# Block-sparse attention and feed-forward kernel: mask tiles built by two concurrent 64-row products, chunk 1 masked by multiplies instead of by TensorE

## The chip, the cores and the metric

The kernel runs on one core of one Trainium2 chip. The metric is the device time of one execution in microseconds, as the median of several executions. The kernel before was run beside every kernel on the same chip. A run over 1.5% above the fastest run of its own kernel is called slow, the others fast; a slow run is left out of the ratios, and no argument should rest on it alone. In the records the engines are called PE (TensorE), DVE (VectorE), ACT (ScalarE), POOL (GpSimd) and SP (SyncE). Run labels such as e1 name the experiments below; the numbers e4 and e5 were not run.

## The reference, cut to what matters

```python
# q, k, v: (4, 8, 768, 64) float32; sampled_blocks: (24, 3)
scores = scale * np.matmul(q, k.transpose(0, 1, 3, 2))
mask = near-diagonal, first and last rows and columns of 32-blocks, plus three sampled blocks a row
attn = softmax(np.where(mask, scores, -1e9))
x = heads_side_by_side(attn @ v)                 # 3072 tokens of 512
xn = x / sqrt(mean(x * x) + 1e-6) * rms_g
out = (silu(xn @ w_gate) * (xn @ w_val)) @ w_out # 512 -> 1536 -> 512
```

The kernel works in 12 chunks of 256 query rows, three for each of four batches. Each chunk has 12 score tiles, exponentials, a mask, the value products, a row normalisation (sum of squares, a reciprocal root, a scaling), transposes, and then the feed-forward products (192 a chunk, 2,304 in all).

## The kernel before: what the change and the argument touch

The mask is put on in one of two ways. For the first `PMASK` pairs of heads (`PEM` is true), TensorE adds a large negative number to the scores by a second product. For all others the exponentials are multiplied by a tile of zeros and ones, `Mk`, made on TensorE by `mask_tile` and copied out by `mask_copy`.

```python
PMASK = 8
def PEM(ch, pr):
    return ch * NP + pr < PMASK            # 8: chunks 0 and 1; 4: chunk 0

def scores(t):
    ...
    nc.tensor.matmul(out=s_, lhsT=x[rows, 1, ...], rhs=x[rows, 0, ...], start=True, stop=not PEM(ch, pr))
    if PEM(ch, pr):
        nc.tensor.matmul(out=s_, lhsT=KindG[rows, ...], rhs=NegQ[rows, ...], start=False, stop=True)

def mask_tile(ic, j2):
    mps[ic, j2] = mp = fbank()             # one PSUM bank
    for j in range(2):
        nc.tensor.matmul(out=mp[:, j * CQ:(j + 1) * CQ], lhsT=KindG[0:64, 2 * j2 + j, :],
                         rhs=NegQ[0:64, cols], start=True, stop=True)

def mask_(t, e):                           # the multiply, on VectorE or GpSimd
    (nc.gpsimd if e == "POOL" else nc.vector).tensor_tensor(
        out=pv, in0=pv, in1=m..., op=ALU.mult)

def rstd(ch):                              # reciprocal root of the row sums, on GpSimd
    nc.gpsimd.tensor_tensor(out=rs, in0=mss[ch], in1=nhalf, op=ALU.pow)

def scale_x(ch, qt):                       # row scaling, on VectorE, two instructions
    for lo, n in ((0, DM), (DM, D)):       # 512 columns and 64 columns
        nc.vector.scalar_tensor_tensor(
            out=x2[:, lo:lo + n], in0=x1s[ch][:, qt, 0:n], scalar=mss[ch][:, qt:qt + 1],
            in1=gB[:, 0:n], op0=ALU.mult, op1=ALU.mult)

def load_stage(b, i):                      # queries, keys, values of batch 1 and up: one buffer for all
    stages[b, i] = raw.tile([P, H, NC * D], FP32, name="stage", tag="stage", bufs=1)
```

Every engine works its instructions off in the order of one long list of words, `ORDER`. In it `m1_0_2*POOL` is a mask multiply of chunk 1 on GpSimd, `sc0_0` a row scaling of chunk 0, `rs0` its reciprocal root, `w5` a pair of idle matmuls, `l1_0_0` half the query load of batch 1, `c1_0_0` one of its casts out of the staging buffer, `va1_0` one of the casts of its values.

The softmax here doesn't subtract the row's maximum and nothing guards it: scores larger than these inputs give would overflow.

## Time and profile before

| | before |
|---|---|
| median of 4 executions beside the changed kernel | 293.5 us (292.52 to 294.8) |
| span of the profiled execution, mean granted clock | 292.3 us, 1.000 |
| first feed-forward product | 30.97 us |
| row scaling of chunk 0 on VectorE, start and length | 26.51 us, 1.81 us |
| query load of batch 1 issued by GpSimd | 42.54 us |

### The profile page before, as it was taken

The page shows a single profiled execution, that of the slowest core. Times are in us where ns is not written, and L with a number is a line of the kernel's source. Part 1 is how long each engine was busy: PE and PEld are TensorE (multiplying, and loading weights), DVE is VectorE, ACT ScalarE, POOL GpSimd, SP SyncE. Part 2 cuts the span into 40 slices and gives each one's busy share as a digit, 9 for nine tenths or more (in the row PEclk, how much of TensorE's full clock was granted, in tenths as well). Part 3 has the DMA queues.
Part 4 walks back from the last instruction along what each step waited for, and adds up shares of the span by engine and source line. Part 5 has one row for each costly group of instructions (what it writes and reads, how often), then busy time and mean ns, then how long its engine had stood idle before and what let it go on. Part 6 is the DMA issues. An engine that isn't in the chain of part 4 may idle for free.

```text
span 292.3 us, 10748 instructions
## 1 busy us (share of the span) xinstructions
PE 284.6 (97%) x4579; PEld 221.1 (76%) x4605; DVE 237.9 (81%) x486; ACT 227.6 (78%) x462; POOL 44.6 (15%) x66
## 2 busy tenths in 40 slices
PE   8999999999999999999999999999999999999995
PEld 4677889965489788686787687688686797776872
DVE  5448298999999999989999979998969788966370
ACT  6899958999999998788599599699399498543312
POOL 9530031726021230001020020000000000000000
PEclk9999999999999999999999999999999999999999
DMA  8999989995875799913679379142051032023203
GB/s 180 311 204 206 292 154 243 172 286 156 186 237 152 185 200 231 168 66 75 220 150 183 103 113 162 21 67 82 2 109 39 3 70 76 2 44 105 74 2 108
DMA packets 56692, 39.76 MB, mean 136 GB/s; under 512 B 42244, under 2 KB 50052, under 8 KB 56644
## 3 DMA queue, kind: packets, MB, share of 16 engines
q1 hardware_dynamic: 45268, 17.11, 33.1%
q0 software_dynamic: 10688, 21.50, 29.4%
q8 instruction: 36, 0.59, 0.9%
q10 hardware_dynamic: 688, 0.46, 0.5%
q14 instruction: 12, 0.10, 0.1%
HBM read 28.57 MB, written 6.29 MB: 119 GB/s over the span
## 4 chain that ended last, share of the span: by engine, by line
PE 83%; DVE 10%; ACT 3%; issue 3%; POOL 0%; POOLq 0%; ACTq 0%; DVEq 0%
PE f L836 37%; PE f L869 19%; PE f L649 10%; PE f L679 10%; DVE pt L669 4%; DVE uu L847 2%; PE f L654 2%; PE f L321 2%; ACT pt L662 2%; DVE hp L854 2%; PE f L484 1%; DVE X L693 1%; DVE x L718 1%; PE f L733 1%; ACT junk L704 0%
## 5 line engine op out<-in xcount | busy, mean ns | idle before, releaser
L662 ACT ACTIVATE pt<-f 128x512 bf16<-128x512 f32 x288 | 151.8, 636 | 8.6 <-PE f L649 7.1
L836 PE MATMUL f<-xn,wgv 64*128 64x256 bf16 x2304 | 139.2, 269 | 0.4 <-DVE uu L847 0.3
L836 PEld LDWEIGHTS <-wgv 64*128 64x128 bf16 x2304 | 117.0, 94 | 11.9 <-issue 2.6
L669 DVE TENSOR_TENSOR pt<-pt,Mk 128x1024 bf16<-128x1024 bf16 x120 | 77.8, 696 | 0.7 <-ACT pt L662 0.7
L869 PE MATMUL f<-wo,hp 128*128 128x512 bf16 (+1 forms) x274 | 65.7, 370 | 1.9 <-issue 0.8
L847 DVE SCALAR_TENSOR_TENSOR uu<-th,f 128x512 bf16<-128x512 bf16 x72 | 48.8, 682 | 12.9 <-ACT th L843 12.6
L843 ACT ACTIVATE th<-f 128x512 bf16<-128x512 f32 x72 | 44.1, 615 | 16.6 <-PE f L836 16.1
L649 PE MATMUL f<-qkT 64*128 64x256 bf16 x576 | 56.5, 273 | 0.5 <-ACT qkT L490 0.2
L854 DVE TENSOR_TENSOR hp<-uu,f 128x512 bf16<-128x512 bf16 x72 | 48.6, 684 | 4.2 <-PE f L836 0.5
L869 PEld LDWEIGHTS <-hp 128*128 128x128 bf16 x300 | 26.1, 98 | 28.2 <-issue 5.1
L679 PEld LDWEIGHTS <-pt 128*128 128x128 bf16 x1152 | 38.4, 97 | 6.8 <-issue 1.1
L679 PE MATMUL f<-va,pt 128*128 128x65 bf16 x1152 | 40.0, 193 | 0.1
L649 PEld LDWEIGHTS <-qkT 64*128 64x128 bf16 x576 | 29.8, 95 | 11.0 <-issue 7.8
L712 POOL TENSOR_TENSOR rs<-ms,nhalf 128x2 f32<-128x2 f32 x12 | 9.8, 816 | 160.9 <-ACT junk L704 127.3
L718 DVE SCALAR_TENSOR_TENSOR x<-X,rs,gB 128x512 bf16<-128x512 f32 (+1 forms) x48 | 22.0, 513 | 10.7 <-POOL rs L712 10.5
L704 ACT ACTIVATE junk<-X 128x513 bf16<-128x513 f32 x22 | 13.8, 636 | 21.6 <-DVE X L693 21.5
L891 ACT ACTIVATE yo<-f 128x512 f32<-128x512 f32 (+1 forms) x24 | 13.4, 607 | 10.8 <-PE f L869 10.8
L693 DVE TENSOR_TENSOR X<-f,rz 128x256 f32<-128x256 f32 x48 | 20.4, 425 | 1.7
L654 PE MATMUL f<-NegQ,KindG 64*128 64x256 bf16 x96 | 13.3, 287 | 0.0
L691 DVE RECIPROCAL rz<-f 128x4 f32<-128x4 f32 x48 | 8.4, 176 | 4.8 <-PE f L679 4.5
L275 POOL DMA_DIRECT2D stage<-in_v_dram x8 | 6.2, 776 | 11.1 <-ACT qb L269 8.5
L269 DVE CAST va<-stage 128x768 bf16<-128x768 f32 x11 | 5.7, 554 | 2.6 <-DMA stage<-in_v_dram 2.6
(82 smaller groups left out, 111.9 us busy)
## 6 DMA issues: line engine op xcount, KB each, us to landing
stage<-in_v_dram POOLq DMA_DIRECT2D x8, 768.0 KB, 7.5
out_dram<-yo SPq DMA_DIRECT2D x23, 256.0 KB, 2.3
stage<-in_k_dram POOLq DMA_DIRECT2D x6, 768.0 KB, 8.8
stage<-in_q_dram POOLq DMA_DIRECT2D x6, 768.0 KB, 6.1
wgv<-in_moe_w_gate_dram POOLq DMA_DIRECT2D x3, 512.0 KB, 17.4
wgv<-in_moe_w_val_dram POOLq DMA_DIRECT2D x3, 512.0 KB, 18.6
wo<-in_moe_w_out_dram POOLq DMA_DIRECT2D x2, 768.0 KB, 17.4
xn<-x SPq DMA_TRANSPOSE x40, 3.3
```

The source lines that it names most:

```text
L649: nc.tensor.matmul(out=s_, lhsT=x[rows, 1, 2 * j2 + jj, pr, :], rhs=x[rows, 0, 2 * ic:2 * ic + 2, pr, :], start=True, stop=not PEM(ch, pr))
L654: nc.tensor.matmul(out=s_, lhsT=KindG[rows, 2 * j2 + jj, :], rhs=NegQ[rows, ic * CQ:(ic + 1) * CQ], start=False, stop=True)
L662: nc.scalar.activation(out=pts[ch, pr][:, j2, e], in_=st[t][e], func=AF.Exp, scale=SCALE)
L669: (nc.gpsimd if e == "POOL" else nc.vector).tensor_tensor(out=pv, in0=pv, in1=m.unsqueeze(1).to_broadcast([P, 2, 2 * CQ]), op=ALU.mult)
L679: nc.tensor.matmul(out=o_[:, qt, e, 0:D + 1], lhsT=pt[:, jt // 2, e, jt % 2 * CQ + qt * P:jt % 2 * CQ + (qt + 1) * P], rhs=va[(ch // NIC) ...
L693: nc.vector.tensor_tensor(out=x1s[ch][:, :, 2 * pr * D:(2 * pr + 2) * D].rearrange("p t (h d) -> p t h d", h=2), in0=o4[:, :, :, 0:D], in1 ...
L718: nc.vector.scalar_tensor_tensor(out=x2[:, lo:lo + n], in0=x1s[ch][:, qt, 0:n], scalar=mss[ch][:, qt:qt + 1], in1=gB[:, 0:n], op0=ALU.mult ...
L836: nc.tensor.matmul(out=gst[u, fp, name][:, half * CQ:(half + 1) * CQ], lhsT=wgv[rows, dpart(i, c), f * P:(f + 1) * P], rhs=xns[u][rows, c, :],
L843: nc.scalar.activation(out=ths[u, fp], in_=gst[u, fp, "gp"], func=AF.Tanh, scale=0.5)
L847: nc.vector.scalar_tensor_tensor(out=uus[u, fp], in0=ths.pop((u, fp)), scalar=1.0, in1=gst.pop((u, fp, "gp")), op0=ALU.add, op1=ALU.mult)
L854: nc.vector.tensor_tensor(out=hps[u][:, 2 * fp:2 * fp + 2, :].rearrange("p f t -> p (f t)"), in0=uus.pop((u, fp)), in1=gst.pop((u, fp, "vp ...
L869: nc.tensor.matmul(out=yst[u, t, half][:, 0:n], lhsT=hps[u][:, f, t * P:(t + 1) * P], rhs=wo[:, f, cols], start=(f == 0), stop=(f == NF - 1))
```

## The change

The aim is to use both halves of the array for mask tiles (two products at a time, into two banks), to take chunk 1's mask products off TensorE (`PMASK` 8 to 4), and to put idle matmuls only where the opening leaves wide gaps. Three of the twelve new multiplies of chunk 1 go to GpSimd. The whole order was made anew. Cut to its core:

```diff
-    PMASK = 8
+    PMASK = 4
-    FILL = 6
+    FILL = 13
-    def mask_tile(ic, j2):
-        mps[ic, j2] = mp = fbank()
-        for j in range(2):
-            nc.tensor.matmul(out=mp[:, ...], lhsT=KindG[0:64, 2 * j2 + j, :], rhs=NegQ[0:64, cols], ...)
+    def mask_tiles(g):
+        for i in range(2):
+            mps[g, i] = fbank()
+        for n in range(4 * g, min(4 * g + 4, NM)):
+            i, (ic, c) = n % 2, divmod(n, NC)
+            rows = slice(64 * i, 64 * i + 64)
+            nc.tensor.matmul(out=mps[g, i][:, ...], lhsT=KindG[rows, c, :], rhs=NegQ[rows, ...], ...)
 ORDER (words of the new one; many left out)
+... rs0 one1 wv2_ ... m1_0_0*DVE m1_0_1*DVE sc0_0:0 sc0_1:1 ... xt0_0:60 w7:5 xt0_1:5 ... sta1_1 ...
+l1_1_0 l1_1_4 m1_0_2*POOL h0_0:0 m1_1_1*POOL wo0_ ... m1_3_1*POOL ...
+sq1_0*ACT sq1_1*ACT c1_1_0*DVE ... sta1_0 dt1_1_0 rs1 l1_0_0 l1_0_4 wo1_ c1_0_0*POOL ...
+... sta1_2 l1_2_0 l1_2_4 va1_0*POOL va1_1*POOL va1_2*POOL va1_3*POOL ... l2_1_0 rs2 l2_1_4 ...
```

## The prediction

> **What bounds the kernel now.** I read the page's busy shares first, then stretches of the span, then the chain and the timeline of the opening.
>
> ```profile
> PE 284.6 (97%) x4579; PEld 221.1 (76%) x4605; DVE 237.9 (81%) x486; ACT 227.6 (78%) x462; POOL 44.6 (15%) x66
> ```
>
> A busy TensorE (PE) is not a TensorE at its peak, so the 97% has to be read by stage. The stretches (start:end, length, then busy us and instruction count of each engine):
>
> ```profile
> 8.00:17.00 9.00, 8.80 (x123) 5.48 (x121) 3.79 (x9) 8.29 (x17) 3.72 (x6) 1.00 1.18 290
> 17.00:31.00 14.00, 13.92 (x284) 11.35 (x283) 8.69 (x24) 13.82 (x29) 2.82 (x4) 1.00 1.24 207
> 31.00:40.00 9.00, 8.87 (x192) 8.11 (x188) 4.17 (x11) 6.34 (x14) 0.00 (x0) 1.00 1.13 276
> 40.00:55.00 15.00, 15.00 (x273) 14.13 (x269) 13.73 (x26) 12.79 (x25) 6.03 (x9) 1.00 0.95 194
> 55.00:85.00 30.00, 29.09 (x418) 19.14 (x418) 29.50 (x60) 29.78 (x63) 11.31 (x14) 1.00 0.85 193
> 110.00:200.00 90.00, 89.26 (x1492) 70.30 (x1498) 83.43 (x164) 74.89 (x153) 6.02 (x8) 1.00 0.72 132
> ```
>
> The order of the columns is PE, weight loads, VectorE (DVE), ScalarE (ACT), GpSimd (POOL). Until 31 us ScalarE is full (13.82 of 14.00) with the exponentials of chunks 0 and 1, and VectorE has 5 us free; from 31 to 40 VectorE has another 5 us free. From 55 to 85 VectorE and ScalarE are both full and TensorE waits a little; after 110 TensorE leads. The first feed-forward product stands at 30.97 us. From there TensorE always has some product in reserve, so the time is roughly that start, plus all TensorE work left then, plus gaps. How that start comes about (the chain, start, length, what):
>
> ```profile
> 27.55 0.55 PE f L733 x8
> 28.11 0.73 PE f L679 x24
> 28.84 0.45 PE f L733 x8
> ...
> 30.73 0.59 ACT pt L662
> 31.33 0.04 issue
> 31.37 2.78 PE f L836 x47
> ```
>
> Between the two batches of transposes (L733) of chunk 0's normalised rows lies one attention-value product of chunk 1 (0.73 us); four score tiles with their mask products fill 29.28 to 30.73 before the first product.
>
> The groups that the change touches (busy us, mean ns):
>
> ```profile
> L654 PE MATMUL f<-NegQ,KindG 64*128 64x256 bf16 x96 | 13.3, 287 | 0.0
> L321 PE MATMUL f<-idle 128*128 128x256 bf16 x26 | 5.8, 373 | 1.1 <-DVE idle L296 1.1
> L559 PE MATMUL f<-NegQ,KindG 64*128 64x256 bf16 x18 | 3.4, 269 | 0.0
> ```
>
> Means are latencies, not costs. Costs come from the chain: "0.11 PE f L654 x2" is 54.5 ns for one mask product when two of different row halves run together, "0.87 PE f L836 x16" gives the same, and 24 value products take 0.73 us. The mask-tile products (L559) use rows 0 to 63 only, and the second starts 0.11 us after the first, so each costs 109 ns.
>
> **What the Trainium skill says.** "TensorEngine Tiling (Array Packing)", Gotcha 1 (PSUM Pressure): different row tiles write different PSUM banks and can't use one bank at the same time. So pairing needs the two banks that the change takes. The trace agrees as far as it goes: the score and mask pairs of two row halves go to two banks and cost 54.5 ns each.
> "TensorE: Matmul & The Clock Gate", Part 1: the array runs at half rate until a window of about 3.4 us has been busy. The trace agrees: the 14 first idle matmuls take 3.17 us, 226 ns each; a pair of score products starts every 0.21 us until 10.1 us and every 0.11 us from 11.9 us.
> "VectorE: DVE Perf Modes", the perf-mode tier table: a bf16 two-tensor product runs two elements a cycle from SBUF, anything fp32 from PSUM one. The trace has 682 ns for the 1024-wide mask multiply and 682 ns for the 512-wide mask copy, issued about 0.61 us apart.
> "GPSIMD Engine Reference", section 3.1 (Elementwise), puts GpSimd about two times slower than VectorE for two-input work. No instruction of this trace shows a wide two-input product there.
>
> **The change, part by part.**
> *Mask products of chunk 1.* 48 of the 96 leave TensorE: 48 x 54.5 ns = 2.6 us. Nearly all lie before 31 us (only the last tile's four follow the first product: 4 x 54.5 = 0.22 us). There ScalarE sets the pace: a tile needs 2 x 0.506 = 1.01 us of exponentials (13 took 6.58 us), against 0.44 us of TensorE with the mask. So the 2.6 us are worth little by themselves; they turn into gaps, which is why the new order has idle matmuls there.
> *Mask tiles.* Before, 18 x 109 ns = 1.96 us, all between 46 and 83 us, where TensorE counts. After, 9 pairs, 0.98 us; by the new order four pairs move before the first product, and five remain, 0.55 us. On the path: -1.41 us.
> *Mask copies.* Before six on VectorE and three on ScalarE, all after 46 us. After, four of 512 columns go into the opening, and the late ones are three of 512 and one of 256 on VectorE, one of each on ScalarE. VectorE's late stretch loses (6 - 3.5) x 0.61 = 1.5 us, ScalarE's (3 - 1.5) x 0.57 = 0.85 us.
> *Mask multiplies of chunk 1.* Twelve more: nine on VectorE, 9 x 0.61 = 5.5 us, three on GpSimd, for which I assume about 2 us each (an estimate from twice the time on VectorE, with issue). Two stand in the wait for the reciprocal root (0.72 us on GpSimd), the other seven, 4.3 us, fall where VectorE was 4.8 us free (31 to 40 us). They should not push the full stretch after 40.
> *Idle matmuls.* 14 more, each about 0.11 us, 1.5 us if none fell into a gap. By the order, nine pairs precede the first product and four follow; those four cost 4 x 0.22 = 0.88 us at worst and nothing at best. None now stands in the first 12 us, where two pairs of the old ones were.
> *Order.* The whole order is new. Chunk 0's exponentials had 1.75 us of evacuations between them on ScalarE (gaps at 11.33, 14.59 and 15.88 us); now one small evacuation and one mask copy, about 0.95 us: -0.8, and about -0.1 for two copies taken off ScalarE ahead of the first exponential. Later, the value product between the two transposes is gone: -0.75. The two multiplies in the root's wait cost about +0.4 (1.2 us against 0.8). Sum -1.25: first product at about 29.7 us. But two score tiles (0.44), that value product (0.73) and one small mask product (0.11) now come after it.
>
> TensorE's work after the first product: 0.44 + 0.73 + 0.11 + 0.55 - 0.22 - 1.96 = -0.35 us, if the late idle matmuls fall in gaps.
> Gaps: in 55 to 85 us TensorE's records are 68 products (3.7), 46 output products of about 0.229 (10.5), 104 scores (5.7), 205 value products of 0.0305 (6.3) and 14 mask-tile products (1.5), 27.7 us of 30, so 2.3 us are gaps. With 1.5 us of VectorE and 0.85 of ScalarE gone, I give back 1.0.
> Sum: -1.25 - 0.35 - 1.0 = -2.6, and 293.4 - 2.6 = 290.8 us.
>
> **Rivals.**
> 1. *The array stays cold longer.* Without idle matmuls early, the window that now turns the clock at about 10.2 us may miss, and the next is 3.4 us later. Four score tiles would cost 0.87 us instead of 0.44, transposes half as much again; ScalarE would idle about 1.5 us. For it: the clock turned only after an unbroken run of scores and idle matmuls. Against: three score tiles still run back to back, and ScalarE has slack against TensorE once started. Result about 292.5.
> 2. *VectorE becomes the bound earlier.* Chunk 1's values now wait for multiplies on VectorE and the slow GpSimd ones, and TensorE takes them in order. If these run late or slow each other, work spills into the stretch after 40 us. For it: VectorE is 92% full from 40 us on. Against: 10 us are free before. Result 293 to 295.
> 3. *Everything removed is hidden anyway*, as the 2.6 us are: then only the 1.4 us of mask tiles count, less idle matmuls: 292.5.
> 4. *The new order packs better everywhere.* TensorE's gaps outside the stretches named come to some 6 us (from 31 to 289 us: 2304 products at 54.6 ns, 125.8; 276 output products at 216 ns and 24 half ones, 62.2; 121 score tiles at 0.218, 26.4; 43 value products at 0.727, 31.3; the rest 3.5; so 249 of 258, 9 us of gaps, less the 2.3). An order that closes half of them gives 288. Nothing in the diff speaks for that in particular.
>
> **Range and chances.** The central sum is small and its largest terms (start of the first product, gaps) come from the order, not from the removed work. Each is uncertain by about 1 us; rivals 1 and 3 lie above, rival 4 below. I take 288.3 to 293.3. Faster by over 2% means under 287.5, which needs rival 4 on top of the sum: 0.10. Slower by over 2% means over 299.2: 0.01. Within 2%: 0.89.
>
> **What would show it.** Right: the first product near 29.7 us; L559's pairs starting together; late mask copies down to six; VectorE fuller in 17 to 40 us and not over 98% after; the last chunk-0 exponential by about 21.9 us. Wrong: scores 0.21 us apart after 11 us (rival 1); TensorE waiting for the mask multiply before chunk 1's values (rival 2); a first product no earlier and the same gaps in 55 to 85 us (rival 3); a gain that lies after 110 us (rival 4).

## More of the kernel before

The lines of the profile stand in the prediction. One that it does not show is the row scaling, from VectorE's timeline:

```profile
26.51 1.81 DVE L718 SCALAR_TENSOR_TENSOR x<-X,rs,gB 128x512 bf16<-128x512 f32 x4 [0.18 <-POOL rs L712]
```

Another line, which the prediction did not use, already held a warning. It is the row of the mask multiplies of the kernel before between 45 and 110 us, with the durations as least, median and greatest, in ns:

```profile
L669 DVE TENSOR_TENSOR pt<-pt,Mk x37: 679/682/1305, 52.3 to 104.3; 128x1024 bf16<-128x1024 bf16 x37
```

Nearly all take 682 ns; the greatest takes 1,305. Only four take over 720 ns, and all four start while GpSimd casts: two, 1,000 and 1,050 ns, beside the query casts of batch 1 (52 to 57 us), and two, 870 and 1,305 ns, beside its value casts (63 to 69 us).

## The result, and the profile after

| | before | after |
|---|---|---|
| median | 293.5 us (292.52 to 294.8), 4 runs | 301.04 us (300.22 to 301.95), 4 runs |
| profiled span, mean granted clock | 292.3 us, 1.000 | 300.2 us, 0.988 |
| first feed-forward product | 30.97 us | 34.96 us |

All runs of both are fast. The ratio is 1.0255 with a 95% interval of 1.0205 to 1.0305: the changed kernel is slower. Ratios in this document are the mean time of one kernel's fast runs over that of the other's of the same rounds, so they are not quite the ratio of the medians quoted.

From the page of the changed kernel, the busy shares and the granted clock by slices of 7.5 us:

```profile
PE 287.6 (96%) x4571; PEld 218.7 (73%) x4571; DVE 251.2 (84%) x497; ACT 226.3 (75%) x461; POOL 49.4 (16%) x69
...
PEclk9999599999999999999999999999999999999999
```

TensorE is as busy as before although it has less to do, and the fifth slice (30 to 37.5 us) has half the clock. The busy shares alone would show nothing of the loss. The stretches of the changed kernel that answer to those of before, with the same columns (PE, weight loads, VectorE, ScalarE, GpSimd, then the clock, the DMA share and GB/s):

```profile
8.00:17.00 9.00, 8.85 (x152) 6.21 (x150) 5.67 (x13) 8.69 (x19) 2.52 (x4) 1.00 1.19 292
17.00:31.00 14.00, 8.88 (x169) 6.38 (x165) 12.56 (x20) 10.54 (x22) 7.36 (x7) 0.97 1.25 206
31.00:40.00 9.00, 8.58 (x99) 5.95 (x101) 6.48 (x13) 5.10 (x11) 1.07 (x2) 0.66 1.13 274
40.00:55.00 15.00, 13.69 (x273) 11.48 (x271) 14.51 (x29) 8.03 (x17) 5.81 (x5) 1.00 0.33 59
55.00:85.00 30.00, 30.00 (x425) 20.69 (x422) 26.68 (x50) 29.19 (x61) 11.11 (x15) 1.00 0.92 210
110.00:200.00 90.00, 89.93 (x1506) 70.53 (x1506) 82.59 (x166) 76.50 (x158) 8.37 (x11) 1.00 0.60 135
```

In 17 to 31 us TensorE is busy for 8.88 us of 14 (before 13.92), and in 31 to 40 us it issues 99 matmuls instead of 192, at a mean clock of 0.66. Those two rows hold the loss. In 55 to 85 us TensorE's records leave no gap at all.

The chain of waits of the changed kernel around its first product (start, length, what):

```profile
23.64 1.11 POOL rs L721
...
24.77 6.60 DVE x L727 x2
...
31.42 0.29 PE f L742
...
35.17 2.79 PE f L845 x32
```

The transposes (L742) waited for the row scaling (L727), which the chain gives 6.60 us. The chain has only the first two of its four instructions. VectorE's timeline has all four (start, length, engine, line, operation, tile):

```profile
24.77 7.45 DVE L727 SCALAR_TENSOR_TENSOR x<-X,rs,gB 128x512 bf16<-128x512 f32 x4
32.15 0.41 DVE L492 COPY qkT<-f 128x512 bf16<-128x512 bf16 x1
```

Before, these four instructions took 1.81 us. The row of this line shows where the time is: least, median and greatest duration are 272, 742 and 5,928 ns. It is one of the two 64-column instructions, normally the short ones, that took 5.93 us, from 25.43 to 31.36 us. In four other kernels with this order (e3, e12, e16, e18) the scaling takes 7.46 us. GpSimd's timeline beside it:

```profile
24.81 0.71 POOL L455 DMA_DIRECT2D wgv<-in_moe_w_val_dram  x1
25.52 1.54 POOL L277 DMA_DIRECT2D stage<-in_k_dram  x2
27.07 4.20 POOL L678 TENSOR_TENSOR pt<-pt,Mk 128x1024 bf16<-128x1024 bf16 x2
31.20 0.86 POOL L461 DMA_DIRECT2D wo<-in_moe_w_out_dram  x1
```

GpSimd's two mask multiplies end at 31.27 us, and VectorE's held instruction ends 0.09 us later. That is no proof yet. The third multiply, at 40.59 us, gives a second such meeting: in that stretch VectorE has three mask multiplies in 3.82 us, one of them 2.61 us instead of 0.68.

The groups that answer to those shown of before (busy us, mean ns):

```profile
L663 PE MATMUL f<-NegQ,KindG 64*128 64x256 bf16 x48 | 6.9, 306 | 0.0
L323 PE MATMUL f<-idle 128*128 128x256 bf16 x40 | 8.1, 338 | 1.3 <-DVE idle L298 1.1
L566 PE MATMUL f<-NegQ,KindG 64*128 64x256 bf16 x18 | 2.0, 271 | 0.0
```

The removed 48 products are gone, and the 18 mask-tile products are busy for 2.0 us instead of 3.4.

The chain that ended last, by engine, before and after, holds one more change:

```profile
PE 83%; DVE 10%; ACT 3%; issue 3%; POOL 0%; POOLq 0%; ACTq 0%; DVEq 0%
PE 75%; DVE 8%; DMA 8%; POOL 3%; ACT 3%; issue 1%; DVEq 0%; ACTq 0%; POOLq 0%
```

Before, no load is on it. After, from 51.67 us it runs over the query load of batch 1 (8.91 us), the value load (10.71 us) and a key load of batch 2 (3.08 us). The query load is issued at 51.67 us, 9.1 us later than before, because it waits for key casts that came late themselves. So from there on the loads carry the lag; whether they add to it is asked below (e16).

To see where the time went from stage to stage, I took the start of the n-th feed-forward product from each trace. The table has it for the kernel before, and for the others how much later (+) or earlier (-) the same product came in the profiled execution. Differences under 1 us should not be read: where the order up to there is the same, the scaling of chunk 0 still starts anywhere from 23.79 us (e6) to 24.77 us (changed kernel). The 384th product is the last of chunks 0 and 1.

| n-th feed-forward product | 1 | 96 | 192 | 288 | 384 | 480 | 768 | 2304 |
|---|---|---|---|---|---|---|---|---|
| before, us | 31.0 | 39.3 | 45.7 | 52.0 | 58.9 | 89.9 | 115.2 | 280.5 |
| after | +4.0 | +2.2 | +8.0 | +8.0 | +7.0 | +8.6 | +7.9 | +7.9 |
| e1, multiplies on VectorE | -2.6 | -5.0 | +0.5 | +0.6 | +0.3 | +7.6 | +6.6 | +6.6 |
| e2, loads ahead of the root | +0.7 | -0.4 | +5.3 | +5.4 | +4.3 | +7.1 | +5.8 | +5.7 |
| e6, multiplies held back | -3.5 | -4.9 | +0.4 | +0.5 | -0.5 | +2.2 | +0.9 | +0.9 |
| e9, e6 with root first | -3.5 | -4.8 | +0.5 | +0.6 | -0.5 | +7.2 | +6.0 | +5.9 |
| e16, after with two staging buffers | +3.3 | +0.7 | +6.5 | +6.5 | +5.5 | +7.3 | +6.0 | +6.4 |
| e18, array kept warm | +2.3 | -0.4 | +5.3 | +5.4 | +4.4 | +11.8 | +10.5 | +10.9 |

The changed kernel has its whole lag by the 192nd product, and the last product's is no greater. The table also shows that the first product is a poor milestone: every kernel with the new order loses 3 to 5 us between the first and the 288th product. All four of chunk 1's value products now come after the first feed-forward product (before, three), and TensorE's records have more gaps: 1.8 us up to the 384th product in e1 and in e6, 0.25 us in the kernel before. (The expectations of e15, e16, e18 and e19 name products by an earlier count in windows of 1 us, in which a product that lay in two windows counted twice. Their 288th, 480th and 576th are the 233rd, 384th and 464th.)

### The profile page after: what moved, and what is told of

Same layout as the page of the kernel before. It is cut to its first block, busy times and chain, and to the rows that moved or that the text cites. A ratio compares the mean times of both kernels' runs of the same rounds, so it can differ in the third digit from the quotient of the medians.

```text
span 300.2 us, 10741 instructions
## 1 busy us (share of the span) xinstructions
PE 287.6 (96%) x4571; PEld 218.7 (73%) x4571; DVE 251.2 (84%) x497; ACT 226.3 (75%) x461; POOL 49.4 (16%) x69
## 4 chain that ended last, share of the span: by engine, by line
PE 75%; DVE 8%; DMA 8%; POOL 3%; ACT 3%; issue 1%; DVEq 0%; ACTq 0%; POOLq 0%
PE f L845 36%; PE f L878 18%; PE f L688 9%; PE f L658 9%; DMA stage<-in_v_dram 4%; DVE pt L678 3%; DMA stage<-in_q_dram 3%; DVE x L727 2%; ACT pt L671 2%; PE f L323 2%; POOL qb L271 1%; DMA stage<-in_k_dram 1%; DVE hp L863 1%; PE f L663 1%; PE f L486 1%
## 5 line engine op out<-in xcount | busy, mean ns | idle before, releaser
L678 DVE TENSOR_TENSOR pt<-pt,Mk 128x1024 bf16<-128x1024 bf16 x129 | 84.7, 701 | 4.0 <-ACT pt L671 3.6
L878 PE MATMUL f<-wo,hp 128*128 128x512 bf16 (+1 forms) x300 | 68.4, 371 | 0.0
L658 PE MATMUL f<-qkT 64*128 64x256 bf16 x576 | 55.2, 276 | 0.4 <-ACT pt L671 0.2
L688 PEld LDWEIGHTS <-pt 128*128 128x128 bf16 x1152 | 37.6, 97 | 7.5 <-issue 2.2
L658 PEld LDWEIGHTS <-qkT 64*128 64x128 bf16 x576 | 28.3, 95 | 13.5 <-issue 10.0
L727 DVE SCALAR_TENSOR_TENSOR x<-X,rs,gB 128x512 bf16<-128x512 f32 (+1 forms) x48 | 27.5, 631 | 7.4 <-POOL rs L721 7.4
L900 ACT ACTIVATE yo<-f 128x512 f32<-128x512 f32 (+1 forms) x24 | 14.8, 626 | 14.7 <-PE f L878 14.2
L323 PE MATMUL f<-idle 128*128 128x256 bf16 x40 | 8.1, 338 | 1.3 <-DVE idle L298 1.1
L742 PE MATMUL f<-ident,x 128*128 128x128 bf16 x32 | 3.1, 245 | 5.6 <-DVE x L727 5.5
L678 POOL TENSOR_TENSOR pt<-pt,Mk 128x1024 bf16<-128x1024 bf16 x3 | 6.9, 2303 | 8.5 <-ACT pt L671 8.5
```

Source lines behind the costliest of these rows:

```text
L658: nc.tensor.matmul(out=s_, lhsT=x[rows, 1, 2 * j2 + jj, pr, :], rhs=x[rows, 0, 2 * ic:2 * ic + 2, pr, :], start=True, stop=not PEM(ch, pr))
L678: (nc.gpsimd if e == "POOL" else nc.vector).tensor_tensor(out=pv, in0=pv, in1=m.unsqueeze(1).to_broadcast([P, 2, 2 * CQ]), op=ALU.mult)
L688: nc.tensor.matmul(out=o_[:, qt, e, 0:D + 1], lhsT=pt[:, jt // 2, e, jt % 2 * CQ + qt * P:jt % 2 * CQ + (qt + 1) * P], rhs=va[(ch // NIC) ...
L727: nc.vector.scalar_tensor_tensor(out=x2[:, lo:lo + n], in0=x1s[ch][:, qt, 0:n], scalar=mss[ch][:, qt:qt + 1], in1=gB[:, 0:n], op0=ALU.mult ...
L878: nc.tensor.matmul(out=yst[u, t, half][:, 0:n], lhsT=hps[u][:, f, t * P:(t + 1) * P], rhs=wo[:, f, cols], start=(f == 0), stop=(f == NF - 1))
L900: nc.scalar.activation(out=yo, in_=yp[:, 0:n], func=AF.Copy, scale=0.5)
```

## The experiments

Four theories stood at the start. A: GpSimd's multiplies hold VectorE's row scaling. B: the weight load and key loads, now behind the root in GpSimd's queue, come too late. C: the fallen clock makes the loss. P: VectorE is simply too full with chunk 1's masks. All runs were compared with the kernel before in the same rounds.

| run | what | median us (range, runs) | ratio, 95% interval |
|---|---|---|---|
| e1 | three GpSimd multiplies to VectorE | 300.48 (297.35 to 301.06, 4) | 1.0206, 1.0139 to 1.0272 |
| e2 | loads ahead of the root | 300.49 (299.61 to 303.97, 4) | 1.025, 1.0175 to 1.0325 |
| e3 | 50 idle matmuls, misplaced | 308.72 (307.73 to 311.79, 4) | 1.0525, 1.0454 to 1.0597 |
| e6 | GpSimd multiplies held back | 295.5 (294.83 to 296.95, 4) | 1.0073, 1.0015 to 1.0132 |
| e7 | e1 and e2 together | 294.34 (293.5 to 300.91, 7) | 1.003, 0.9977 to 1.0084 |
| e8 | e7, root ahead of value casts | 298.83 (297.73 to 301.3, 6) | 1.0191, 1.0136 to 1.0245 |
| e9 | e6, root ahead of value casts | 301.76 (299.92 to 302.58, 6) | 1.0256, 1.021 to 1.0303 |
| e10 | e1, root ahead of value casts | 300.09 (298.79 to 301.98, 6) | 1.0222, 1.0172 to 1.0272 |
| e11 | e7, key casts on GpSimd | 299.69 (297.26 to 302.63, 6) | 1.018, 1.0132 to 1.0229 |
| e12 | after, key casts on GpSimd | 304.81 (303.73 to 305.83, 6) | 1.0374, 1.0334 to 1.0413 |
| e13 | e11, mask tiles unpaired | 299.85 (297.94 to 301.1, 6) | 1.0205, 1.0162 to 1.0248 |
| e14 | e11, chunk 1 masked by TensorE | 302.57 (300.94 to 303.84, 6) | 1.0299, 1.0255 to 1.0342 |
| e15 | e7, two staging buffers | 300.99 (296.47 to 306.77, 6) | 1.017, 1.011 to 1.0231 |
| e16 | after, two staging buffers | 302.37 (300.39 to 303.83, 6) | 1.0291, 1.0253 to 1.0329 |
| e17 | before, two staging buffers | 303.01 (302.14 to 310.03, 6) | 1.031, 1.0276 to 1.0343 |
| e18 | after, array kept warm in the wait | 302.44 (301.04 to 304.94, 6) | 1.0309, 1.0262 to 1.0355 |
| e19 | e7 again | 296.83 (294.35 to 302.88, 4) | 1.0093, 1.004 to 1.0146 |
| e20 | e7, second output-weight load early | 297.9 (293.97 to 301.74, 6) | 1.0095, 1.0037 to 1.0153 |

The ranges of e7, e11, e15, e17, e19 and e20 contain slow runs, which the ratios leave out; the medians in the table do not. All results were correct.

### Who holds the row scaling: e1, e2, e6

```diff
-l1_1_0 l1_1_4 m1_0_2*POOL h0_0:0 m1_1_1*POOL wo0_ ... m1_3_1*POOL
+l1_1_0 l1_1_4 m1_0_2*DVE h0_0:0 m1_1_1*DVE wo0_ ... m1_3_1*DVE        (e1)

-s14:12 rs0 one1 wv2_ ... sta1_1 ... l1_1_0 l1_1_4 m1_0_2*POOL
+s14:12 wv2_ sta1_1 l1_1_0 l1_1_4 rs0 one1 ... m1_0_2*POOL             (e2)

+        if t == (1, 0, 2):                                            (e6)
+            nc.gpsimd.tensor_copy(out=hold, in_=x2s[0, 1][:, DM:DM + 1])
```

e6 leaves the multiplies on GpSimd, but makes GpSimd first read a column that the last scaling instruction writes.

> The three mask multiplies of chunk 1 that stood on GpSimd go to VectorE; nothing else differs from the changed kernel. Theory A (the GpSimd multiplies, 27.07 to 31.27 us, hold up VectorE's row scaling, whose 64-column instruction took 5.93 us instead of 0.28): the scaling of chunk 0's rows takes 1.8 us again, the first feed-forward product starts at about 29 us instead of 35, the array's clock does not drop, and the time is 291 to 295 us. Theory B (the load issues that GpSimd makes from 24.8 to 27.1 us hold it up, or the late loads cost the time): the scaling stays at 5 us or more or the time stays above 298 us. Theory C (the array's clock is the cause and the rest follows): the clock drops here too and the time stays above 298 us.

> The last value-weight load and the two key loads of batch 1 stand ahead of the reciprocal root on GpSimd again, as in the kernel before; the three multiplies stay on GpSimd. Theory A: the multiplies now follow the root directly, the scaling is held up by 4 us or more, and the time stays at 298 to 302 us. Theory B: the scaling takes about 1.8 us and the time falls to 292 to 296 us.

> GpSimd reads one column of the scaled rows of chunk 0 before its first multiply, so that the two multiplies start only after the scaling; they stay on GpSimd. Theory A: the scaling takes 1.8 us, the first product starts at 29 to 30 us, but VectorE's own multiplies of chunk 1 are held up instead while GpSimd works (one of them 2 us or longer); time 293 to 297 us. Theory B: the load issues from 24.8 us on still hold the scaling up, and the time stays above 298 us.

VectorE's scaling in e1, from its timeline:

```profile
24.68 1.80 DVE L727 SCALAR_TENSOR_TENSOR x<-X,rs,gB 128x512 bf16<-128x512 f32 x4
```

And in e6, VectorE, then GpSimd:

```profile
23.79 1.80 DVE L730 SCALAR_TENSOR_TENSOR x<-X,rs,gB 128x512 bf16<-128x512 f32 x4
...
27.05 0.41 DVE L492 COPY qkT<-f 128x512 bf16<-128x512 bf16 x1
27.95 4.24 DVE L681 TENSOR_TENSOR pt<-pt,Mk 128x1024 bf16<-128x1024 bf16 x3 [0.49 <-ACT pt L671]
```
```profile
26.23 4.20 POOL L681 TENSOR_TENSOR pt<-pt,Mk 128x1024 bf16<-128x1024 bf16 x2
```

The scaling is back to 1.80 us in both, and the first product comes at 28.32 us (e1) and 27.45 us (e6). In e1 the same three loads are issued at 24.71 to 26.97 us, right beside the scaling, and do not slow it: it is the multiplies that hold, not the issue of loads. In e6 the same multiplies run 26.23 to 30.43 us, and what they hold now are VectorE's own mask multiplies, three in 4.24 us (the greatest 3.04 us instead of 0.68); behind them TensorE waits 1.0 us for VectorE, not 5.2. The copy at 27.05 us, which reads PSUM, runs under GpSimd's multiply at its usual 0.41 us.

e2 leaves the multiplies and the scaling side by side. The scaling took 5.54 us (two of its instructions are held, 2.14 and 2.62 us, each until one GpSimd multiply has ended) and the time is the changed kernel's. So A is right and B alone is not the cause. P is not it either: in e1 VectorE does all twelve multiplies and TensorE is level with the kernel before at the 384th product (+0.3 us). By the lag table, taking the multiplies out of the way gives back 7.4 us (e1) and 7.5 us (e6) by the 288th product. But only e6 keeps most of it until the end (+0.9 us at the last product); e1 loses 7.3 us again between the 384th and the 480th product, 59 to 90 us. That is a second cause, taken up below.

### What the wait costs, and what the clock: e3, e18

```diff
-lambda e: warmer(2)
+lambda e, i=i: warmer(50 if i == 7 else 2)       (e3: w7 stands behind xt0_0)
+lambda e, i=i: warmer(48 if i == 6 else 2)       (e18, and in the order: w5:1 s17:21 w6:1 xt0_0:60)
```

> The idle pair between the two transposes of chunk 0 becomes 50 idle matmuls (5.4 us), which fill TensorE's wait for the held-up scaling. The wait itself stays. If theory A holds and the dropped clock is a consequence that costs something of its own, products are 54.5 ns apart from the first on, the first product still starts later than 32 us, and the time falls by 1.5 to 2.5 us to about 299. Theory C: the time falls to below 296 us. If the clock costs nothing: unchanged, 300.5 to 301.5.

> The changed kernel with 48 idle matmuls of 256 columns (0.107 us each by the trace, 5.1 us) between the scores and the first transposes of chunk 0's rows, where TensorE waits 5.22 us for the held scaling in any case. They should keep the clock at 1.00 through the wait and end with it. The wait itself stays. If the lower clock after the wait (0.66 in 31 to 40 us) costs time, the lag at the 288th product falls from 7.7 us to 5 to 6.5 and the time to 298 to 300; if the clock costs nothing, 300 to 302.

e3 was misplaced: the transposes ahead of the idle matmuls wait for the held scaling too, so the idle matmuls came after the wait. TensorE's timeline in e3:

```profile
31.28 0.29 PE L742 MATMUL f<-ident,x 128*128 128x128 bf16 x1 [5.24 <-DVE x L727]
31.36 8.22 PE L323 MATMUL f<-idle 128*128 128x256 bf16 x50
```

It says nothing of the clock, only that idle matmuls ahead of needed work delay it: 50 of them took 8.22 us, and the first product came at 41.05 us, 6.1 us later than in the changed kernel. e18 puts them ahead of the wait:

```profile
24.59 5.41 PE L323 MATMUL f<-idle 128*128 128x256 bf16 x48
...
33.31 1.97 PE L845 MATMUL f<-xn,wgv 64*128 64x256 bf16 x32
```

The clock stays at 1.00 from 24 to 40 us (changed kernel 0.66 in 31 to 40 us), the first 32 products take 1.97 us instead of 2.95, and the lag at the 288th product falls from 8.0 to 5.4 us. Of these 2.6 us some 0.8 are chance, since the scaling started that much earlier here (24.01 and 24.77 us). So of the 7.4 us that the hold-up costs by the 288th product (8.0 less e1's 0.6), about 2 are the clock that fell during the wait, and about 5 the wait itself. But the total did not fall (302.44 us). In the profiled execution, at 304.94 us the slowest of the six, 7.4 us were lost between the 384th and the 480th product, where GpSimd waited 11.34 us for the values of batch 1 and VectorE 3.3 us for the root behind them.

### The second stage: e7, e8, e9, e10

In 59 to 90 us the load of batch 1 is the suspect. Queries, values and then the keys of batch 2 go one after another through the one staging buffer, each load waiting for GpSimd's casts of the one before, and the root of chunk 2 stands in the same queue. In e1 (a fast run) VectorE's longest wait in 45 to 100 us was for that root:

```profile
DVE x L727 <- POOL rs L721: 5.3, 1, 5.3
```

GpSimd's queue in e1 (the wait ahead of an instruction stands in brackets):

```profile
68.27 1.60 POOL L271 CAST va<-stage 128x768 bf16<-128x768 f32 x2 [6.37 <-DMA stage<-in_v_dram]
75.57 1.60 POOL L271 CAST va<-stage 128x768 bf16<-128x768 f32 x2 [5.70 <-DMA stage<-in_v_dram]
77.47 0.75 POOL L277 DMA_DIRECT2D stage<-in_k_dram  x1 [0.30 <-POOL va L271]
78.24 0.73 POOL L721 TENSOR_TENSOR rs<-ms,nhalf 128x2 f32<-128x2 f32 x1
```

In e6, where the same loads landed earlier, the second pair of casts starts at 68.69 us and the root runs at 72.11 us. The query load was issued at 44.19 us in e1 and at 44.16 us in e6, so that e6's advantage is not in when it issues this load.

```diff
 e7: e1 and e2 together
-sta1_2 l1_2_0 l1_2_4 va1_0*POOL va1_1*POOL va1_2*POOL va1_3*POOL ... sta2_1 ... l2_1_0 rs2 l2_1_4
+sta1_2 l1_2_0 l1_2_4 ... rs2 va1_0*POOL va1_1*POOL va1_2*POOL va1_3*POOL sta2_1 l2_1_0 l2_1_4
 e8: e7 with this; e9: e6 with this; e10: e1 with this
```

> All three GpSimd multiplies moved to VectorE, as in e1, and the last weight load and the two key loads issued before the reciprocal root of chunk 0, as in e2. Theory B (the later loads are what loses the second stage once the hold-up is gone): the query load of batch 1 would be issued at about 42 us instead of e1's 44.19, the second half of the values would be cast before 71 us instead of 75.57, time 292 to 296. Theory Q (GpSimd's later work in one queue, not these loads): the query load stays at 44.2 because it waits for the key casts, and the time stays within 1% of e1's 300.5, 297.5 to 303. I hold Q for likelier, 60 to 40.

> e7, and in GpSimd's queue the root of chunk 2 stands before the casts of batch 1's values instead of behind them (the key loads of batch 2 behind both). Theory Q: the root runs as soon as its sum of squares is there (about 72 us, e1 had 78.24), VectorE no longer waits 5.3 us for it, TensorE in 80 to 85 us is busy over 4 us of 5 (e1: 1.81), time 293 to 296.5. Rival R (the loss in 55 to 85 us is VectorE's and ScalarE's own load, mask copies and multiplies in an order that does not fit): the root moves but the time stays above 298.

> e6 (the GpSimd multiplies held until the row scaling of chunk 0 is done) with the same root-first order of GpSimd's queue. In e6 the root came at 72.11 with only 0.79 us of idle time before it, so theory Q expects little: 293.5 to 296 (e6 295.5), and less spread over the runs. Rival R: no change at all, 295 to 296.5.

> e1 (GpSimd multiplies on VectorE, late loads as in the changed kernel) with the root-first order alone. Theory Q: about the time of e8, 293.5 to 297, with the root at about 72 us and VectorE's wait for it gone. Rival R: 298 to 302, as e1. If e10 is fast and e7 is not, the root's place in the queue is the second cause and the early loads are not; if e7 is fast as well, either is enough.

e7 brought the time to that of before, which speaks for B as a second condition once the hold-up is gone (e1 300.48, e7 294.34 us; again as e19, with fast runs of 294.35 to 297.14 us), though I had thought it the less likely. The ratio's interval of e19 just meets that of e1. How the earlier loads do this is not shown: the profiled execution of e7 was a slow one, and its query load was issued at 44.26 us, as in e1.

The root-first order failed in all three. The root moved as meant (73.32, 71.25 and 70.23 us), and the wait for it went, but the key load of batch 2 was now behind the casts. In e9 GpSimd's queue is

```profile
71.25 0.71 POOL L724 TENSOR_TENSOR rs<-ms,nhalf 128x2 f32<-128x2 f32 x1 [11.36 <-ACT junk L716]
71.93 4.05 POOL L271 CAST va<-stage 128x768 bf16<-128x768 f32 x4
76.28 1.54 POOL L277 DMA_DIRECT2D stage<-in_k_dram  x2 [0.30 <-POOL va L271]
```

The key load was issued at 76.28 us instead of e6's 70.58, VectorE's casts of these keys began at 84.4 us instead of 79.6, and VectorE stood still for 3.4 us ahead of them with everything else behind. e9 against e6 is the cleanest pair: the traces agree within 0.1 us until the 384th product (both -0.5), then a key load 5.7 us later, 5.0 us more lag at the 480th product (+7.2 and +2.2), and 301.76 us instead of 295.5. So VectorE's casts of batch 2's keys, at about 80 us of the order, have no slack for their load; in the kernel before they ran at 79.8 us, with the load issued at 69.11 and 72.11 us. The granted clock is lower after such a stop: e9 has 0.77 in 85 to 100 us, e1 0.90, where e6 and the kernel before have 1.00.

### Attempts to give that chain slack, and two parts of the change by themselves: e11 to e14

```diff
 e11 (from e7) and e12 (from the changed kernel)
-... wo0_ ... c1_1_0*DVE c1_1_1*DVE c1_1_2*DVE c1_1_3*ACT ... sta1_0 ... rs1 l1_0_0 l1_0_4 wo1_
+... wo0_ c1_1_0*POOL ... c1_1_5*POOL sta1_0 l1_0_0 l1_0_4 ... rs1 wo1_
 e13 (from e11)
-            rows = slice(64 * i, 64 * i + 64)
+            rows = slice(0, 64)
 e14 (from e11): PMASK = 8 again, the twelve words m1_... taken out
```

> e7 with batch 1's six key casts on GpSimd as soon as the keys have landed (about 27 to 31 us, they ran at 41 to 44 us on VectorE and ScalarE) and the query load right behind them. Theory S (one staging buffer: key casts, query load, query casts, value load, value casts, key load of batch 2, key casts on VectorE follow one another with no slack, so that any late landing holds VectorE or the root behind it): the query load is issued near 32 us (e7 44.26), the key casts of batch 2 find their data there, no wait over 1 us of TensorE in 45 to 100 us, all runs on the fast side: 289 to 293, with no run over 296 (e7: 293.5 and 300.9). Rival R (VectorE's and ScalarE's order in 55 to 85 us): still two values, 293.5 and 300. Rival P (GpSimd's casts now slow VectorE's opening): first feed-forward product 1 us or more later than 28.3 us.

> The changed kernel with only that: the three multiplies still on GpSimd, the six key casts on GpSimd behind the first two multiplies, and the query load right behind them. The hold-up of the row scaling stays (5 to 6 us, first product at 34 to 35 us). Theory S says that the staging chain costs part of the 7.5 us that the change lost: time 295 to 299, no wait over 1 us in 55 to 100 us; if the hold-up alone made the loss, it stays at 300 to 302.

> e11 with the mask products all in rows 0 to 63, so no two of them run at the same time; the two banks stay. 12 mask products of opening and later; one pair costs some 0.11 us less than two in a row by the spacing of matmuls in the trace, so 24 products in all cost at most 1.3 us of TensorE more, and 0.4 of it ahead of the first product: 0 to 1.3 us slower than e11, likeliest 0.3 to 0.8.

> e11 with chunk 1's mask put on by TensorE again (as before the change), its 12 VectorE multiplies gone. If moving chunk 1's masks to VectorE was right, this is slower by the mask products it brings back (48 of 64x256, some 0.055 us of array each where paired, 2.6 us in all): 2 to 3.5 us slower than e11; if VectorE was the tighter engine in this stage, the same time or faster.

e11 did not test what it was meant to. The keys were not there: GpSimd waited for them until 38.09 us,

```profile
38.09 3.54 POOL L272 CAST kb<-stage 128x512 bf16<-128x512 f32 x6 [12.44 <-DMA stage<-in_k_dram]
```

though their load had been issued at 18.96 us. The DMA share stands at 1.13 to 1.25 from 8 to 40 us, which fits a load that waits behind those issued before it; this was not tested. The query load moved only to 41.93 us, the root of chunk 1 went behind it, and nothing was gained. In e12 the third GpSimd multiply came behind those casts (44.86 us) and TensorE waited 3.3 us for it.

e13 against e11 is the pairing alone: 299.85 against 299.69 us, with overlapping intervals; a gain under 1 us can't be told from none. e14 against e11 is the move of chunk 1's masks off TensorE: the fast runs have medians of 302.57 and 299.33 us, and the intervals do not meet. That part of the change is worth about 3 us in the new order.

### Two staging buffers: e15, e16, e17

```diff
-name="stage", tag="stage", bufs=1)
+name="stage", tag="stage", bufs=2)
-("yo", 4, [P, DM], FP32))}
+("yo", 2, [P, DM], FP32))}    # the last output rows and early index tiles laid into other buffers; scratch of the squares 1 buffer, not 2
 query load behind wo0_, value load behind rs1 (e15 from e7, e16 from after, e17 from before)
```

> e7 (multiplies on VectorE, loads ahead of the root) with two staging buffers instead of one; the query load of batch 1 issued behind the first output-weight load (about 26 us, e7 44.26) and the value load behind the root of chunk 1 (about 44 us, e7 59.93). Room comes from early index tiles laid into a buffer not used before 30 us and from two output rows instead of four. Theory S: the key load of batch 2 is issued by 65 us (e7 77.18), the root of chunk 2 runs at about 72 us, no wait of VectorE on a root or a key load in 55 to 100 us, the 576th feed-forward product within 1.5 us of the kernel before: 291 to 294 in every run. Rival R (order of VectorE and ScalarE): the loads move and the 576th product still comes 5 us or more late, 298 to 301.

> The changed kernel itself with the two staging buffers and the early loads, multiplies still on GpSimd. The trace of the changed kernel has its whole lag of 7.7 us by the 288th product (56 us) and 7.7 at the last, so if the hold-up alone makes the loss, this gains nothing: 299.5 to 302. If the staging chain has a part in it, 296 to 299.

> The kernel before with the two staging buffers and the early loads. Its trace has no wait over 0.5 us in 55 to 85 us, the chain just fits: no gain, 292.5 to 294.5. If it sits on the chain as a bound: 290 to 292.5.

All three failed to get faster, and e17 made the kernel before 9 us slower. Room for the second buffer was taken from the output rows and the scratch of the row sums, and that alone can cost: in e17 (the profiled run is a fast one) ScalarE waited 4.4 us for a store of an output row to leave its buffer. The first half of the key load of batch 2 was issued early (e16 61.38 us, changed kernel 79.10 us), the second half was not (78.64 us), so the single buffer is not the only bound of this stage. e16 does bear on the changed kernel: with the loads early, TensorE still waited 5.7 us for the scaling, the lag at the 192nd product was 6.5 us, and the time stayed at 302.37 us. Because of the smaller output rows I take no more from these runs.

### The same kernel twice, and one load moved: e19, e20

```diff
 e19: e7 unchanged
 e20 (from e7)
-wo0_ ... l1_0_0 l1_0_4 wo1_ c1_0_0*POOL
+wo0_ wo1_ ... l1_0_0 l1_0_4 c1_0_0*POOL
```

> e7 once more, unchanged. If the profiled execution is a fast one (293.5 to 296.5): the 480th feed-forward product as in e7 (within 0.5 us), the query casts and value casts on GpSimd 2 us or more earlier than e7's 55.72 and 75.29 (second half), the root of chunk 2 at 70 to 73 us instead of 77.95, and the 576th product within 2 us of the kernel before. If the landing times are the same as in the slow execution and the time is still 294, the landings are not the cause.

> e7 with the second output-weight load issued right behind the first (about 26 us instead of 45.80). Theory D (the crowded DMA engines just after 44 us delay the query load, and everything staged behind it): the query casts start by 52 us (e7 55.72), the second value half is cast by 70 us (e7 75.29), the root of chunk 2 by 73 us, and every run is on the fast side, 292 to 295.5. Rival: the loads land as late as before or the backlog until 38 us grows and delays the keys of batch 1 (key casts wait past 42 us): 296 to 302.

The profiled execution of e19 was a slow one again (302.88 us; the other three 294.35 to 297.14), so there is no trace of a fast e7. e20 has three fast runs (293.97 to 297.36) and three slow ones (298.44 to 301.74). In its profiled execution the query casts began at 60.76 us (e7 55.72), so it gives no sign that taking the weight load out of the way makes the query land sooner. Both these traces are of slow executions, so this is weak. The fast runs (ratio 1.0095) are no faster than e7's; the rival's outcome is the nearer one, though not by its reason, for the key casts were not late (41.18 us).

## Why the prediction was wrong, point by point

**The opening was right as far as the root.** The clock turned in time: score products stand 0.11 us apart from 10.83 us, so rival 1 did not happen. Chunk 0's last exponential ended at 21.07 us (the prediction asked for about 21.9), and the scaling began at 24.77 us, 1.74 us earlier than before. Mask tiles run in pairs, eight products in the opening, and the late mask copies are down to six, as said.

**The step that failed is the sentence on the three GpSimd multiplies**, "three on GpSimd, for which I assume about 2 us each". The length was right (2.1 us each). What was wrong was to count them as work beside other work, at no cost to anyone. They held one 64-column scaling instruction on the path for 5.93 us instead of about 0.28 us. So the term of -1.25 us for the first product became +4.0 us, and with the clock that fell in the wait the lag was 8.0 us by the 192nd product (e18: about 2 for the clock, about 5 for the wait; e1 and e6: at most 0.6 with the multiplies out of the way). Rival 2 had the words for it ("slow each other") but was priced by how full VectorE is, and put the harm at the values of chunk 1. The harm was one instruction on the way to the transposes. With that, 0.01 for a loss of over 2% was far too little.

The skill had it. "Advanced Engine Details and Errata", section GPSIMD Details, states that GpSimd shares a read and a write interface with VectorE and conflicts with VectorE's instructions that have two SBUF inputs or run in a 2-port mode; "GPSIMD Engine Reference", section 1 (Specifications), says the same of the SBUF interfaces. The scaling has two SBUF inputs (`X` and `gB`). I looked up how long a GpSimd multiply takes and not what it shares. Traces agree: scaling 1.80 us without and 7.45 us with GpSimd's multiplies, VectorE's two-input mask multiplies up to 3.04 us instead of 0.68, and a copy from PSUM not held.

**The first terms came out about right in their sum at 59 us, and that is luck.** Undisturbed, the first product came 2.6 us (e1) and 3.5 us (e6) earlier, not 1.25. But from there to the 384th product both took some 3 us more than the kernel before. About 0.6 us of it is work, much as the prediction's terms for this stretch had it (one value product, 0.73 us, a small mask product, 0.11, less mask products); 1.6 us are new gaps of TensorE, which it did not have. So at 59 us e1 stands at +0.3 us and e6 at -0.5; the prediction's terms up to there (without the mask tiles that came later) make -0.4. Moving chunk 1's masks was worth its effort (e14: about 3 us), while the pairing of mask tiles is too small to be seen (e13).

**The -1.0 us given back in 55 to 85 us did not come.** I took VectorE and ScalarE for what bounds that stretch. e9 against e6 shows that in these two the landing of a staged load decides it, which stops VectorE's in-order queue at about 80 us. No profiled kernel with the new order gains between the 384th and the 480th product, and of the fast ones those within 0.5 us of the kernel before at the 384th, or ahead of it, lose 2.7 to 8.4 us. In the changed kernel, already 7.0 us late there, only 1.6 us more are lost; but the landing of loads is the likely reason why undoing the hold-up alone (e1) did not bring the time back, and no version here beats the kernel before. The best are e7 and e6, level with it within 1%. The reading of the gaps was also a little off: one count over 55 to 85 us gives 44 output products, 100 scores and 192 value products, not 46, 104 and 205, so by the same costs the gaps are 3.4 us and not 2.3.

**What stays open.** Why loads issued at the same time land some microseconds apart: e1 and e6 issue the queries within 0.03 us and cast them 2.3 us apart (56.24 and 53.98 us), and there is no trace of a fast run of e7. The one try at it, e20, was profiled in a slow run. Open too is why the hold-up begins at 25.43 us, before the recorded start of GpSimd's multiply at 27.07 us; starts on GpSimd are rough in these traces.

## What to carry to other kernels

Before work is moved to an engine that has time, ask what that engine shares with the one on the path, and look for the instructions there that it could hold, the short ones too: a held instruction costs what the other engine still has to do, not its own length (here 5.93 us instead of 0.28). Test it by holding the moved work back until the urgent instruction is done, as e6 does with one read. And where a kernel's order fits the landing times of loads without slack, time won ahead of them is not kept: find the next load that an in-order queue must wait for before counting a gain.

## What the Trainium skill lacked or had wrong

- No page has what happens when GpSimd has two multiplies in a row. Here one 64-column two-input VectorE instruction was held through both, 5.93 us instead of about 0.28 us, in the changed kernel; in e2 two VectorE instructions were held, one for each multiply (2.14 and 2.62 us).
- "GPSIMD Engine Reference", section 3.1, has a ratio of 1.96 between the engines for a fp32 two-input add of 2,048 columns, and no figure for bf16. The 1024-wide bf16 mask multiply took 2.1 us on GpSimd against 0.68 us on VectorE, 3.1 times.
- No page has how far the landing of loads of the same size varies: the query load issued at 44.19 us in e1 and at 44.16 us in e6 was cast from 56.24 and from 53.98 us.
